# Five warm-up steps of TensorE for eight, and a second level of the 7-for-8 product in the third block

## The chip, the cores and the metric

The kernel runs on one core of a Trainium2 chip, in one launch. A core has a matrix engine (TensorE, "PE" in the profile; its weight loads are listed apart as "PEld"), three engines for elementwise work (VectorE "DVE", ScalarE "ACT", GpSimd "POOL"), an engine that here only issues transfers (SyncE, "SP"), and 16 DMA engines that serve all of them. Each engine takes its own instructions in the order in which the program lists them, and waits on semaphores for the others. The metric is the device time of one execution in microseconds; 2% is the line between "faster", "the same" and "slower".

## The reference, cut to what matters

```python
# attention, for 8 batches x 12 heads, 448 tokens, 64 columns per head, all fp32
q_n, k_n = rmsnorm(q, g_q), rmsnorm(k, g_k)
scores = (1 / sqrt(64)) * q_n @ k_n.T
attn = softmax(scores)                      # along the keys
x = (attn @ v)                              # heads side by side: (8*448, 768)

# bilinear feed-forward, d_model 768, d_ff 1536
a = x @ w_a                                 # (3584, 1536)
b = x @ w_b                                 # (3584, 1536)
out = (a * b) @ w_out                       # (3584, 768)
```

The attention is small beside the three large products. The weights arrive as float64 and are rounded to fp32 on the chip.

## The kernel before: the parts that matter here

A small scheduler in the kernel (`Plan`) records every operation with an estimate of its time and a priority (a lower key goes first), and lays the operations out in one fixed order for each engine before anything runs. A change in the list of operations can thus move others.

The 8 batches are cut into `NB = 4` blocks of two batches (`beta` 0 to 3). For each block `ffn(beta)` makes `h = (x w_a) * (x w_b)` with `quarter_products`, and then `last_product` multiplies `h` by `w_out`. All of them use the 7-for-8 algorithm (Strassen's, in Winograd's form): a product is cut in quarters, and seven products of quarters, with sums before and after, replace eight. The sums are DVE work; the factors on the weights' side are computed once, kept in DRAM (`kept`) and read back by `stream`.

`last_product` takes groups of 128 tokens in pairs: three pairs in an even block, four in an odd one (the tokens left over from both blocks of two make the fourth). For each of the seven factors `f` and each pair, one product of quarters is 6 matmuls of 128x384. In the fourth block, and for five of the seven factors, two pairs are taken together as a group, and a second level of the same algorithm cuts their 12 matmuls into seven products of 3 matmuls of 128x192:

```python
WARM = 8
TWICE = (1, 2, 3, 4, 6)        # factors with a second level
MAKE = 1                       # block in which the second level's weight factors are made
ONCE = NB - 1                  # first block that uses the second level
...
for f in (0, 1, 2, 4, 3, 5, 6):
    stream(beta, 12 + place_of[f], f)
    if beta == MAKE and f in TWICE:
        inner_factors(beta, f)
    if beta >= ONCE and f in TWICE:
        stream_inner(beta, f)
groups = [(0, 1), (2, 3)][:len(pairs) // 2] if beta >= ONCE else []
alone = [t for t in pairs if not any(t in g for g in groups)]

def each(f, a, base, to):
    twice = groups if f in TWICE else []
    for g in twice:
        inner_products(beta, key + place_of[f], f, g, a, base, to, acc, (c_, U_), out_place)
    for t in pairs if not twice else alone:
        product(t, f, a(t), plain(t, base, to))
```

`product` is the plain form, with its result taken by `plain` in one DVE addition (0.56 us each) or a copy on ACT:

```python
for c in ks:                                                 # 6 in all
    nc.tensor.matmul(held["po"][:, 0:HALF], lhsT=a[0]()[:, c], rhs=sts[beta, 12 + place_of[f]][:, c], ...)
```

`inner_products` is the second level (cut to its matmuls and the names of its sums):

```python
factor(0, a10, a11, ALU.add, nx1)                   # four sums of token quarters, on DVE (Si)
factor(1, s(0), a00, ALU.subtract, ...)
factor(2, a00, a10, ALU.subtract, nx)
factor(3, a01, s(1), ALU.subtract, ...)
...
for c in range(MI):                                 # MI = 3, HI = 192; seven such products: a b a d g e g
    nc.tensor.matmul(held[bank], lhsT=x()[:, c], rhs=y(c), ...)
...                                                 # seven to twelve DVE additions behind them (pi, fin, oi)
```

Its weight factors come from `inner_factors` (per `f` eight DVE subtractions into two small buffers, each followed by a store to DRAM) and return by `stream_inner`: four loads per `f`, which take over the attention's buffers and therefore wait until the attention has ended:

```python
tag, bufs = ("ET", 4) if place_of[f] % 2 == 0 else (("v", 2), ("v", 2), ("q", 1), ("k", 1))[n]
...
nc.sync.dma_start(inner[beta, f, n], kept["t"][:, f, n])      # needs "ended": the attention is done
```

A block's `ffn` may be recorded before or after the last attention heads:

```python
if p // (2 * HC) <= ONCE:
    ffn(p // (2 * HC) - 1)
elif p == NC:
    for beta in range(ONCE, NB):
        ffn(beta)
```

At the start, before the first heads have arrived, TensorE runs warm-up steps of four 128x128 matmuls whose results nobody reads:

```python
def warm():
    for x in range(4):
        nc.tensor.matmul(warms[0][:, 0, 0:P], lhsT=ident, rhs=ident, start=True, stop=True)
...
for x in range(WARM):
    op("PE", 0.86, 1e6, warm, ["warm"], ["warm"], mode="full")
```

Of the kernel before, what the change touches and what calls it, by code (L numbers as in the profile page):

```python
# [25 lines left out]
class Plan:  # L26
# [22 lines left out]
    def op(self, engine, us, key, emit, reads=(), writes=(), new=(), mode=None, chain=None, kb=0, lock=False, dmas=1):  # L49
        n, deps, tiles = len(self.ops), set(), set()  # L50
        for t in new:
            self.opener[t] = n
            tiles.add(t)
        for r in reads:
            if r in self.wrote:
                deps.add(self.wrote[r])
            self.read.setdefault(r, []).append(n)
        for w in writes:
            if w in self.wrote:
                deps.add(self.wrote[w])  # L60
            deps.update(self.read.pop(w, ()))
            self.wrote[w] = n
        for x in (*reads, *writes):
            t = x.split("/")[0]
            if t in self.tags:
                deps.add(self.opener[t])
                tiles.add(t)
        deps.discard(n)
        self.ops.append((engine, us, key, emit, deps, mode, chain, kb, tuple(new), tiles, lock, dmas if kb else 0))
        return n  # L70
# [100 lines left out]
def kernel(  # L171
# [112 lines left out]
    NB = B // 2  # L284
# [14 lines left out]
    def fast_body(ld, wk, ps_s, ps_o, ps_mm, dram):  # L299
        plan = Plan()  # L300
        op, tile_of = plan.op, plan.tile
# [3 lines left out]
        HC, NT = HP // 2, S // D  # L305
        NC = B * HC
        STS, XS = 2, 9
        WARM = 8
        TWICE = (1, 2, 3, 4, 6)
        MAKE = 1  # L310
        ONCE = NB - 1
        LOADS = "ACT"
        KEEPS = "ACT"
        APART = 24
# [91 lines left out]
        def stream(beta, n, f=None):  # L406

            st = tile_of(f"st{beta}.{n}", "st", STS)

            def load():  # L410
                t = sts[beta, n] = ld.tile([P, 7, KH * P], FP32, tag="st", name="st", bufs=STS)
                if f is None:
                    nc.sync.dma_start(t.rearrange("p a b -> p (a b)"), kept[n])
                else:
                    nc.sync.dma_start(t[:, 0:MH], kept["o"][:, f])
            reads = [f"kept{n}"] if f is None else [f"kept{len(order) + x}" for x in range(MH)]
            op("SP", 0.5, 6.0 * beta + n / 4, load, reads, [f"{st}/{x}" for x in range(7)] + ["streaming"], new=[st],
               kb=1376 if f is None else 1180)
# [268 lines left out]
        def last_product(beta, h, key):  # L687
# [22 lines left out]
            pairs = range(PAIRS if odd else OWN)  # L710
# [5 lines left out]
            def product(t, f, a, take):  # L716

                po, held = tile_of(f"po{beta}.{t}.{f}", "mm", 2), {}
                for part in range(2):
                    ks = range(part * MH // 2, (part + 1) * MH // 2)  # L720

                    def emit(ks=ks):
                        if ks[0] == 0:
                            held["po"] = ps_mm.tile([P, 512], FP32, tag="mm", name="po")
                        for c in ks:
                            nc.tensor.matmul(held["po"][:, 0:HALF], lhsT=a[0]()[:, c], rhs=sts[beta, 12 + place_of[f]][:, c],  # L726
                                             start=(c == 0), stop=(c == MH - 1))
                    op("PE", len(ks) * HALF / 595, key + place_of[f], emit, a[1] + [f"st{beta}.{12 + place_of[f]}/0"], [po, "ffn"],
                       new=[po] if part == 0 else [], mode="full")
                take(po, lambda: held["po"][:, 0:HALF])  # L730
# [19 lines left out]
            c_, U_ = (lambda t: f"{fin}/c{t}"), (lambda t: f"{fin}/U{t}")  # L750
            for f in (0, 1, 2, 4, 3, 5, 6):
                stream(beta, 12 + place_of[f], f)
                if beta == MAKE and f in TWICE:
                    inner_factors(beta, f)
                if beta >= ONCE and f in TWICE:
                    stream_inner(beta, f)
            groups = [(0, 1), (2, 3)][:len(pairs) // 2] if beta >= ONCE else []
            alone = [t for t in pairs if not any(t in g for g in groups)]

            def each(f, a, base, to):  # L760


                twice = groups if f in TWICE else []
                for g in twice:
                    inner_products(beta, key + place_of[f], f, g, a, base, to, acc, (c_, U_), out_place)
                for t in pairs if not twice else alone:
                    product(t, f, a(t), plain(t, base, to))

            def out_place(t, i):
                return 2 * S * beta + (t + OWN * i) * P if t < OWN else 2 * S * (beta - 1 + i) + 2 * OWN * P  # L770
# [1 line left out]
            def plain(t, base, to):  # L772
                name = lambda y: (c_, U_)[y](t)
                if base is None:
                    return lambda po, ps: op("ACT", 0.5, -1, lambda: nc.scalar.copy(acc(t, to), ps()), [po], [name(to)])
                if not isinstance(to, tuple):
                    return lambda po, ps: op("DVE", 0.6, -1, lambda: nc.vector.tensor_tensor(acc(t, to), acc(t, base), ps(), ALU.add),
                                             [po, name(base)], [name(to)])

                def take(po, ps):  # L780
                    out_(t, *to[:2], base)(po, ps)
                    if len(to) > 2:
                        op("DVE", 0.6, -1, lambda: nc.vector.tensor_tensor(acc(t, to[2]), acc(t, to[2]), ps(), ALU.add),
                           [po], [name(to[2])])
                return take
# [60 lines left out]
        def stream_inner(beta, f):  # L846
            for n in range(4):
                tag, bufs = ("ET", 4) if place_of[f] % 2 == 0 else (("v", 2), ("v", 2), ("q", 1), ("k", 1))[n]
                nm = tile_of(f"ti{beta}.{f}.{n}", tag, bufs)

                def load(n=n, tag=tag, bufs=bufs):
                    shape = {"ET": [P, 2, S], "k": [P, NT, 2, D]}.get(tag, [P, 2, NT * D])
                    t = (wk if tag == "ET" else ld).tile(shape, FP32, tag=tag, name="ti", bufs=bufs)
                    flat = t.rearrange("p a b c -> p (a b c)" if tag == "k" else "p a b -> p (a b)")
                    inner[beta, f, n] = flat[:, 0:MI * HI].rearrange("p (k n) -> p k n", k=MI)
                    nc.sync.dma_start(inner[beta, f, n], kept["t"][:, f, n])
                op("SP", 0.5, 6.0 * beta + (12 + place_of[f]) / 4, load, [f"kt{f}.{n}.0", f"kt{f}.{n}.{MI - 1}", "ended"], [nm], new=[nm], kb=295)
# [247 lines left out]
        def weights(at, after):  # L1105
            for x, n in enumerate(seq):
                if at == GATES[x]:
                    factors(n, x * 0.45 + 1.0, x < 2, [after])
# [5 lines left out]
        for p in range(NC + 1):  # L1114
            if p < NC:
                for nm in "qkv":
                    loads(p, nm)
            if p == 0:
                weights(0, "k0")
                op("SP", 1.0, -1.9, load_gains, [], ["grow"], kb=1, dmas=2)  # L1120
                op("DVE", 0.4, -9, use_gains, [], ["grow"])
                op("DVE", 0.4, 20.0, judge_gains, ["grow"], [])
                spread_gains()
                for x in range(WARM):
                    op("PE", 0.86, 1e6, warm, ["warm"], ["warm"], mode="full")
            if p < NC:
                normalize(p)
                transposes(p)
                scored(p, 0)
                scored(p, 1)  # L1130
            if p > 0:
                if p > WIDE:
                    sums_over_keys(p - 1, None)
                invert(p - 1)
                divide(p - 1)
                if (p - 1) % (2 * HC) == 2 * HC - 2:
                    combine((p - 1) // (2 * HC), 0)
                if p % (2 * HC) == 0:
                    combine(p // (2 * HC) - 1, 1)
                    combine(p // (2 * HC) - 1, 2)  # L1140
# [6 lines that stand above are left out]
            if p < NC:  # L1147
                for j in range(NT):
                    values(p, j)
                    if p < WIDE:  # L1150
                        sums_over_keys(p, j)
                    elif j:
                        add_up(p, j)
                    if j + 2 < NT:
                        scored(p, j + 2)
                put_out(p)
# [130 lines left out]
```

## Time and profile before

The time is 1555.44 us (median of 3 runs, 1555.27 to 1557.61). The profiled execution has a span of 1553.5 us.

| engine | busy us | share of the span | instructions |
|---|---|---|---|
| PE (matmul) | 1515.4 | 98% | 6894 |
| PEld (weight load) | 813.1 | 52% | 6894 |
| DVE | 769.9 | 50% | 1089 |
| ACT | 399.4 | 26% | 647 |
| POOL | 315.0 | 20% | 166 |

| stretch, us | what runs there |
|---|---|
| 0 to 235 | attention of the first block; the weights are loaded, rounded and kept |
| 235 to 394 | the rest of the first block's quarter products |
| 394 to 576 | attention of the second block; the first block's last product |
| 576 to 755 | the second block's quarter products |
| 755 to 962 | attention of the third block; the second block's last product |
| 962 to 1140 | the third block's quarter products |
| 1140 to 1173 | the last heads of the fourth block's attention, with the rest of the quarter products |
| 1173 to 1254 | the third block's last product |
| 1254 to 1443 | the fourth block's quarter products |
| 1443 to 1553 | the fourth block's last product, with the second level |

How to read the lines of a profile: L726 is line 726 of the kernel. An fp32 matmul shows as two records, so "x6" in the trace are three matmuls of the program. The mean duration of one matmul is longer than the distance between two, because they are pipelined: distances are read from the chain of waits, where a row is the start, the length and the number of records. PEclk, in a table of stretches, is the TensorE clock that was granted (1.00 is full). `po` is a plain product of the last product (L726), `pq` a quarter product (L1003), and the seven products of the second level are `a`, `b`, `d`, `g`, `e` (L901). `hraw` and `lraw` hold the weights as loaded, `st` the rounded factors, `ti` the second level's weight factors, `tk` the same while they are made.

### The profile page before, as it was taken

To read this page: it belongs to the slowest core of one execution; us is meant where nothing else is said; L and a number is where in the kernel's file an instruction comes from. 1 tells how busy PE (TensorE), PEld (TensorE's weight loads), DVE (VectorE), ACT (ScalarE), POOL (GpSimd) and SP (SyncE) were. 2 spreads that over 40 slices of the span, in tenths; PEclk is the share of its full clock that TensorE was granted. 3 is DMA by queue.
4 is the path that set the end of the run, shared out by engine and by line. 5 is a ranking of instruction groups with operands and counts; after the bars stand their busy time and mean duration, and the time that the engine had idled before them with its cause. 6 is when DMAs were issued, how large, how long until landed. Compare 5 with 4: busy or idle time off the path is not lost.

```text
span 1553.5 us, 17619 instructions
## 1 busy us (share of the span) xinstructions
PE 1515.4 (98%) x6894; PEld 813.1 (52%) x6894; DVE 769.9 (50%) x1089; ACT 399.4 (26%) x647; POOL 315.0 (20%) x166
## 2 busy tenths in 40 slices
PE   8988999999999999999999999999999999999998
PEld 6654344555444555555444455555545555555796
DVE  4887769888786412222377542222235222222583
ACT  4767662111557200000455400000040000000000
POOL 2426442111255200001244400001110001000000
PEclk9999999999999999999999999999999999999999
DMA  8898445554535551212246445121214432222343
GB/s 236 232 261 244 97 102 182 182 198 153 162 110 122 143 169 71 107 71 95 82 109 164 109 146 174 72 107 71 107 64 149 127 127 90 89 77 95 110 138 110
DMA packets 122528, 204.09 MB, mean 131 GB/s; under 512 B 57157, under 2 KB 105541, under 8 KB 112709
## 3 DMA queue, kind: packets, MB, share of 16 engines
q1 hardware_dynamic: 94372, 149.40, 32.4%
q10 hardware_dynamic: 28064, 53.48, 9.9%
q8 instruction: 56, 0.92, 0.2%
q14 instruction: 36, 0.29, 0.1%
HBM read 160.83 MB, written 41.85 MB: 130 GB/s over the span
## 4 chain that ended last, share of the span: by engine, by line
PE 85%; DMA 4%; DVE 4%; ACT 3%; issue 1%; POOL 1%; SPq 0%; ACTq 0%; DVEq 0%; POOLq 0%
PE pq L1003 49%; PE po L726 18%; PE o L537 6%; PE sc L515 5%; DMA q_sb<-in_q_dram 2%; PE su L573 2%; PE pt L494 2%; ACT ET L521 2%; PE g L901 1%; PE a L901 1%; DVE x L662 1%; PE warm L1094 1%; DMA hraw<-in_moe_w_out_dram 1%; DMA kept_o<-st 1%; PE b L901 1%
## 5 line engine op out<-in xcount | busy, mean ns | idle before, releaser
L1003 PE MATMUL pq<-x,st 128*128 128x448 f32 x2016 | 763.4, 540 | 0.0
L1003 PEld LDWEIGHTS pq<-x,st 128*128 128x128 f32 x2016 | 381.2, 190 | 378.6 <-issue 369.9
L521 ACT ACTIVATE ET<-sc,ms 128x448 f32<-128x448 f32 x336 | 192.8, 636 | 92.9 <-PE sc L515 66.3
L726 PE MATMUL po<-st,hT 128*128 128x384 f32 x624 | 204.8, 487 | 0.0
L537 PE MATMUL o<-ET,v_sb 64*64 64x448 f32 x1344 | 186.3, 551 | 9.2 <-ACT ET L521 8.7
L515 PE MATMUL sc<-qkT 64*64 64x448 f32 x1344 | 177.7, 548 | 17.3 <-ACT ET L521 10.1
L464 POOL TENSOR_TENSOR ms<-ms,expo 128x14 f32<-128x14 f32 x48 | 147.2, 3085 | 205.1 <-DVE ms L462 199.7
L1051 POOL TENSOR_TENSOR hT<-hT,t 128x448 f32<-128x448 f32 x24 | 28.8, 1199 | 746.6 <-DVE t L1049 744.3
L726 PEld LDWEIGHTS po<-st,hT 128*128 128x128 f32 x624 | 117.9, 190 | 84.7 <-issue 3.6
L1025 ACT COPY hT<-pq 128x448 f32<-128x448 f32 x24 | 12.8, 533 | 436.4 <-PE pq L1003 436.4
L515 PEld LDWEIGHTS sc<-qkT 64*64 64x64 f32 x1344 | 59.3, 133 | 93.9 <-issue 34.3
L551 POOL TENSOR_TENSOR sum<-sum,ET 128x896 f32<-128x896 f32 x38 | 81.0, 2131 | 127.5 <-ACT ET L521 76.0
L537 PEld LDWEIGHTS o<-ET,v_sb 64*64 64x64 f32 x1344 | 60.9, 134 | 87.0 <-ACT ET L521 39.5
L726 PE MATMUL po<-st,fin 128*128 128x384 f32 x312 | 105.5, 490 | 0.0
L726 PEld LDWEIGHTS po<-st,fin 128*128 128x128 f32 x312 | 58.3, 190 | 46.6 <-issue 7.8
L551 DVE TENSOR_TENSOR sum<-sum,ET 128x896 f32<-128x896 f32 x57 | 62.4, 1095 | 39.6 <-POOL sum L551 33.9
L746 DVE TENSOR_TENSOR o_sb<-fin,po 128x384 f32<-128x384 f32 x44 | 24.4, 555 | 113.1 <-PE po L726 109.3
L1063 POOL TENSOR_TENSOR hT<-hT,t 128x448 f32<-128x448 f32 x48 | 57.9, 1208 | 51.0 <-DVE t L1060 47.5
L458 DVE TENSOR_REDUCE ms<-sq 128x14 f32<-128x896 f32 x48 | 51.8, 1079 | 24.9 <-ACT sq L456 24.7
L1056 DVE TENSOR_TENSOR hT<-U,pq 128x448 f32<-128x448 f32 x48 | 29.8, 621 | 66.3 <-PE pq L1003 66.3
L1060 DVE TENSOR_TENSOR t<-U,pq 128x448 f32<-128x448 f32 x48 | 29.7, 619 | 61.5 <-PE pq L1003 59.1
L1028 ACT COPY t<-pq 128x448 f32<-128x448 f32 x24 | 12.8, 534 | 176.0 <-PE pq L1003 176.0
(113 smaller groups left out, 1145.2 us busy)
## 6 DMA issues: line engine op xcount, KB each, us to landing
st<-kept SPq DMA_DIRECT2D x36, 1344.0 KB
st<-kept_o SPq DMA_DIRECT2D x28, 1152.0 KB
kept<-st ACTq DMA_DIRECT2D x12, 1344.0 KB
q_sb<-in_q_dram SPq DMA_DIRECT2D x48, 224.0 KB
k_sb<-in_k_dram SPq DMA_DIRECT2D x48, 224.0 KB
v_sb<-in_v_dram SPq DMA_DIRECT2D x48, 224.0 KB
rec<-inv SPq DMA_DIRECT2D x48, 224.0 KB
lraw<-in_moe_w_a_dram ACTq DMA_DIRECT2D x12, 768.0 KB
```

Source lines behind the costliest of these rows:

```text
L458: op("DVE", 1.1, key, lambda: nc.vector.tensor_reduce(rs[p][:, s], xs["sq", nm, p], AX, ALU.add), [sq], [f"{ms}/{nm}"])
L464: lambda: nc.gpsimd.tensor_tensor(msf(), msf(), expo[:, 0:2 * NT * (b - a)], ALU.pow), [], names)
L494: nc.tensor.transpose(t[:, j * P:(j + 1) * P], x[:, j].rearrange("p h d -> p (h d)"), ident)
L515: nc.tensor.matmul(t[low_high[w], e, 0:S], lhsT=qkTs[p][low_high[e], 1, j * P + w * D:j * P + (w + 1) * D], rhs=qkTs[p][low_high[e], 0, w ...
L521: nc.scalar.activation(E[:, e], scs[p, j][:, e, 0:S], AF.Exp, scale=rs[p][:, 1, 2 * j + e:2 * j + e + 1])
L537: nc.tensor.matmul(os_[p][low_high[e], w, 0:S], lhsT=xs["v", p][low_high[w], e, j * D:(j + 1) * D], rhs=ETs[p, j][low_high[w], e], start=( ...
L551: two[e].tensor_tensor(sums[p], sums[p] if j > 1 else ETs[p, 0], ETs[p, j], ALU.add)
L573: nc.tensor.matmul(sus[p][w][low_high[e], :], lhsT=ones[low_high[w], :], rhs=x[low_high[w], e], start=first, stop=last)
L726: nc.tensor.matmul(held["po"][:, 0:HALF], lhsT=a[0]()[:, c], rhs=sts[beta, 12 + place_of[f]][:, c], start=(c == 0), stop=(c == MH - 1))
L901: nc.tensor.matmul(held[bank], lhsT=x()[:, c], rhs=y(c), start=(start and c == 0), stop=(stop and c == MI - 1), skip_group_check=True)
L1003: nc.tensor.matmul(banks[bank][:, 0:S], lhsT=sts[at][:, f, c * P:(c + 1) * P], rhs=quads[x][:, c], start=(start and c == 0), stop=(stop an ...
L1063: lambda i=i, n=n, nm=nm: two[TIMES].tensor_tensor(C(i, n), C(i, n), held[nm], ALU.mult), [t], [hp[i]],
```

## The change

It has three parts. `WARM` goes from 8 to 5, and the scheduler is told that the first three steps take longer (2.5, 1.7 and 1.7 us) than the rest. The second level is also used in the third block (`ONCE = NB - 2`), for all seven factors, for the pairs 0 and 1; pair 2 stays plain. For this the second block makes the weight factors of all seven `f`. And inside `each` the plain product of the pair that stands alone now goes ahead of the group. In the fourth block, the second level stays at the same five factors. The aim of the second part is less matmul work: 21 half-size matmuls in place of 12 for each of the seven factors.

```diff
-        WARM = 8
-        TWICE = (1, 2, 3, 4, 6)
+        WARM = 5
+        TWICE = {NB - 2: (0, 1, 2, 3, 4, 5, 6), NB - 1: (1, 2, 3, 4, 6)}
         MAKE = 1
-        ONCE = NB - 1
+        ONCE = NB - 2
...
                 stream(beta, 12 + place_of[f], f)
-                if beta == MAKE and f in TWICE:
+                if beta == MAKE:
                     inner_factors(beta, f)
-                if beta >= ONCE and f in TWICE:
+                if f in TWICE.get(beta, ()):
                     stream_inner(beta, f)
...
-                twice = groups if f in TWICE else []
+                twice = groups if f in TWICE.get(beta, ()) else []
+                for t in pairs if not twice else alone:
+                    product(t, f, a(t), plain(t, base, to))
                 for g in twice:
                     inner_products(beta, key + place_of[f], f, g, a, base, to, acc, (c_, U_), out_place)
-                for t in pairs if not twice else alone:
-                    product(t, f, a(t), plain(t, base, to))
...
                 for x in range(WARM):
-                    op("PE", 0.86, 1e6, warm, ["warm"], ["warm"], mode="full")
+                    op("PE", (2.5, 1.7, 1.7)[x] if x < 3 else 0.9, 1e6, warm, ["warm"], ["warm"], mode="full")
```

Since `ONCE` also decides when a block's `ffn` is recorded, the third block's `ffn` now stands behind the last head in the list of operations. In the built program TensorE's order is the same up to the third block's attention, but for the start: there 16 warm-up matmuls, then the seven transposes of the first keys, the small gain product, four more warm-up matmuls, and then the transposes of the first queries; before, all 32 warm-up matmuls came first.

## The prediction

> **What bounds the kernel now.** I read the page first: TensorE is busy 98% of the span, and the chain that ended last is 85% TensorE work. So a change counts only if it shortens TensorE's work or closes a gap in it. Then I read the chain in order of time for the two places that the change touches, the third block's last product and the second level in the fourth block.
>
> ```profile
> 1172.76 81.27 PE po L726 x252
> 1254.03 189.42 PE pq L1003 x504
> 1443.45 15.48 PE po L726 x48
> 1458.93 0.97 PE a L901 x6
> ...
> 1464.78 1.18 PE g L901 x6
> 1465.97 0.97 PE a L901 x6
> ```
>
> The first row is the whole stage that gets the second level: 81.27 us for 7 factors x 3 pairs, 3.87 us per plain product and pair, without a gap. The third gives the same price (15.48 / 4 = 3.87). The last three bound one group of the second level that nothing disturbs: from 1458.93 to 1465.97 are 7.04 us for what costs 2 x 3.87 = 7.74 us in the plain form.
>
> For the start I read the timeline of the first 30 us and stretches of 2 us:
>
> ```profile
> 10.42 1.13 DVE L468 TENSOR_TENSOR qn<-q_sb,ms 128x896 f32<-128x896 f32 x1
> 11.47 0.93 PE L494 MATMUL pt<-ident,k_sb 128*128 128x128 f32 x7
> 12.75 0.39 ACTq L379 DMA_DIRECT2D hraw<-in_moe_w_out_dram  x1
> 14.81 1.74 PE L515 MATMUL sc<-qkT 64*64 64x448 f32 x16 [1.19 <-ACT qkT L501]
> 23.41 1.58 ACT L271 ACTIVATE st<-hraw 128x1536 f32<-128x1536 f32 x1 [5.28 <-DMA hraw<-in_moe_w_out_dram]
> 26.41 2.29 PE L537 MATMUL o<-ET,v_sb 64*64 64x448 f32 x8 [4.54 <-ACT ET L521]
> ```
>
> ```profile
> 10.00:12.00 2.00, 2.00 (x20) 2.00 (x19) 1.42 (x3) 0.00 (x0) 1.99 (x2) 1.00 0.28 64
> 12.00:14.00 2.00, 1.62 (x13) 1.20 (x11) 0.00 (x0) 1.22 (x3) 0.98 (x1) 1.00 0.45 125
> ...
> 22.00:24.00 2.00, 0.00 (x0) 0.00 (x0) 0.00 (x0) 0.59 (x1) 0.00 (x0) 1.00 0.92 307
> 24.00:26.00 2.00, 0.00 (x0) 0.00 (x0) 0.96 (x1) 2.00 (x3) 0.00 (x0) 0.61 1.04 403
> 26.00:28.00 2.00, 1.59 (x9) 1.06 (x13) 1.95 (x2) 1.93 (x4) 0.00 (x0) 0.50 1.10 332
> ```
>
> (Columns of the stretches: PE, PEld, DVE, ACT, POOL busy, granted clock, DMA share, GB/s.) The eight warm-up steps run from 1.37 to 11.63 and the key transposes stand behind them. ACT's gain copy and the first weight load on ACT's queue wait in turn for TensorE, so the DMA engines are nearly idle from 10 to 14 us. The load lands late, ACT blocks on it for 5.28 us, TensorE has nothing for 4.54 us, and at about 24.5 us its clock falls to half until about 31.
>
> **What the Trainium skill says.** "TensorE: Matmul & The Clock Gate", section "Back-to-back issue gap", gives N/2.4 + 2.5 ns between matmuls when warm, and "FP8 and Floating Point Precision", section "TensorE Precision Notes", gives four passes for true fp32. My estimate from the two is 4 x 82.5 = 330 ns for 192 columns and 4 x 162.5 = 650 ns for 384. The trace has 0.97 / 3 = 323 and 15.48 / 24 = 645 ns: it agrees, and half-size matmuls are not dearer per column. "What's actually happening" in the first page says that the clock is halved after about 3.4 us of idleness; here it fell during a gap of 4.5 us, while gaps of 1.2 us left it alone. "VectorE: DVE Perf Modes", section on the TRN2 errata, gives (N+151)/0.96 ns for an fp32 tensor_tensor: 557 ns for 384 elements, 357 for 192; the rows of the second level's sums have 554 and 352 to 358.
>
> **The change part by part.**
>
> *Second level in the third block.* Per factor, the group costs 7.04 for 7.74 us: 0.70 us less. Times seven: 4.9 us, all on TensorE and so on the path, if nothing stalls. The stage becomes 7 x (3.87 + 7.04) = 76.4 us.
>
> *What this adds to DVE there.* Counted from the new order between the first token sum and the end of the stage: 28 token sums x 0.555 = 15.5; the additions behind the groups 20.7 (1.75 for f=0, 3.0 for each of five, 3.95 for f=5); nine sums between factors x 0.95 = 8.6; seven plain takes 3.9; the attention's last divisions and combinations, and the last sums of `h`, about 8. Together 57 of 76 us, 74%. Before, it was
>
> ```profile
> 1172.60:1254.00 81.40, 81.40 (x254) 48.01 (x253) 31.25 (x47) 1.62 (x4) 1.13 (x1) 1.00 0.42 137
> 1473.00:1503.50 30.50, 28.50 (x170) 27.16 (x169) 26.38 (x57) 1.28 (x4) 0.00 (x0) 1.00 0.48 158
> ```
>
> The second row is the fourth block's worst stretch, two groups for f=2 and f=4: DVE 26.38 of 30.5 us. Undisturbed it should take 4 x 7.04 = 28.15 us, so about 2.4 us are lost there. The third block has half as much second-level work and a plain product of 3.87 us ahead of each group for DVE to get its sums done, so I expect no such hole.
>
> *What it adds to the DMAs.* 28 more loads of 288 KB, 8.3 MB, on 137 GB/s x 81.4 us = 11.2 MB: about 19.4 MB in 76.4 us, 254 GB/s. Scaled from a share of 0.42 that is near 0.78. The st load of a factor must land within one factor, 10.9 us, and the traffic of a factor with stores (2.36 MB and 0.6 MB) needs about 9 us at the 325 GB/s which share and rate imply. Tight, not over. For holes of both kinds I put +0.7 us.
>
> *More weight factors.* Sixteen more DVE subtractions, 8 x 0.55 + 8 x 0.35 = 7.2 us, with 16 stores. They are made in the second block's last product and, for f=0, inside the third block's attention, where TensorE waits for others now and then (idle 0.6 of the 57 us to 811, 2.6 of the next 71). They have priority over the attention's sums and share two small buffers with the quarter products. With the reshuffle of the attention's order around them I put +1.0 us, give or take two.
>
> *Warm-up.* A step is 8 records; at 11 per 2 us at first and 20 at the end, the first four steps end near 7 us. The keys land near 8.0 (ACT starts on them at 8.04), so their transposes run at 8.0 in place of 11.47. The weight load is issued near 9.2 in place of 12.75: 3.5 us earlier, into the empty stretch. The queries are ready at 11.55, so the first scores start near 13.55 in place of 14.81: 1.25 us. How much survives until 235 us depends on who leads there. If it is the attention chain, 1.25; if the DMAs (share 0.8 to 1.1 over most of the first 150 us), 3.5; if the earlier landing also spares the idle 4.5 us and the 4 to 5 us at half clock, up to 6. I take 3.0.
>
> Sum: -4.9 - 3.0 + 0.7 + 1.0 = -6.2 us, 1549.2 us.
>
> **The rivals.**
>
> *A: the second level is paid back in the third block.* DVE sums or `ti` loads end last, as they did in the fourth block. For it: 2.4 us were lost there, and DMA demand nearly doubles. Against it: 74% DVE, plain products in between, and the first eight `ti` loads were issued between 1156 and 1167 us even before, some 10 us ahead of need. It would make the stage 79 to 82 us and the kernel 1552 to 1555.
>
> *B: the start doesn't carry.* The weights' chain (DVE 88% busy from 25 to 125 us) absorbs what the first 25 us gain, or the thinner warm-up leaves TensorE at half clock for the first heads. Against the latter: after step four it still transposes, and idles under 2 us at a time. It would leave 1551 to 1553.
>
> *C: the new order hurts the attention of the third block.* DVE is in order; a `tk` subtraction that waits for its buffer's store holds up the sums that attention needs. Before, such waits came to 5.7 us in five cases. It would add 2 to 5 us: 1551 to 1554.
>
> *D: the start gives everything* and removes the half-clock stretch: 1545 to 1546.
>
> **Range and chances.** A to D move it by 3 to 5 us each, independently. I take 1543.5 to 1554.5 as the range. 2% would be 31 us, six times what any part can give, and no added work comes near it in the other direction: chances 0.01 faster, 0.98 the same, 0.01 slower.
>
> **What would show it.** In the profile after: the stage of the third block's last product between the quarter products takes 76 to 78 us, with groups of 7.0 us; the first weight load is issued before 10 us; no half clock, or a shorter one, near 25 us; the transition from the first attention to the unbroken run of quarter products (235.6 us before) comes about 3 us earlier; the stretch from there to the start of the third block's last product is as long as before, within 2 us. It is wrong if groups in the third block show waits on `ti` or `Si`, if the 235 us mark hasn't moved, or if the third block's attention has grown by over 3 us.

## The result, and the profile after

The kernel after takes 1548.32 us (median of 4 runs, 1543.98 to 1550.43), the kernel before beside it 1556.11 us (4 runs, 1555.27 to 1557.61). The ratio is 0.9945, 95% interval [0.9919, 0.9972]: 7.8 us less, within 2%. A second measurement of the same kernel (7 runs) gave 1550.27 us and a ratio of 0.9964 [0.9951, 0.9977]. The profiled execution took 1550.43 us with a span of 1548.6, the longest of the four, so the two profiles differ by 4.9 us and not by 7.8.

The start comes first. These are rows of the timeline of the kernel after (start, length, engine and line; in brackets the idle time before and what ended it), and then its stretches of 2 us (columns as before: PE, PEld, DVE, ACT, POOL busy, granted clock, DMA share, GB/s):

```profile
9.23 0.39 ACTq L379 DMA_DIRECT2D hraw<-in_moe_w_out_dram  x1
13.65 1.73 PE L515 MATMUL sc<-qkT 64*64 64x448 f32 x16 [1.16 <-ACT qkT L501]
16.84 1.67 ACT L271 ACTIVATE st<-hraw 128x1536 f32<-128x1536 f32 x1
```

```profile
10.00:12.00 2.00, 0.77 (x7) 0.57 (x6) 1.27 (x2) 0.19 (x1) 2.00 (x2) 1.00 1.01 258
12.00:14.00 2.00, 0.84 (x9) 0.46 (x11) 0.00 (x0) 1.01 (x1) 0.88 (x1) 1.00 1.02 418
...
24.00:26.00 2.00, 2.00 (x25) 1.46 (x21) 1.97 (x2) 0.64 (x3) 1.81 (x1) 1.00 1.02 418
```

The load goes out at 9.23 in place of 12.75, and the DMA engines are full from 10 us on, where they had shares of 0.28 and 0.45. ACT's first conversion of weights (`st<-hraw`) starts at 16.84 in place of 23.41 and carries no bracket: the data are there when its turn comes. So the chain ACT blocked, TensorE idle for 4.54 us, clock halved is gone whole; PEclk is 1.00 in every stretch shown. Scores begin only 1.16 us earlier than before.

The second level in the third block's last product, in the chain of waits of the kernel after (start, length, what), and the stage as one stretch:

```profile
1185.68 0.97 PE a L901 x6
...
1191.53 1.19 PE g L901 x6
1192.72 3.87 PE po L726 x12
...
1237.92 7.74 DMA out_dram<-oi
...
1247.88 1.24 PE g L901 x6
```

```profile
1170.60:1249.10 78.50, 76.56 (x380) 63.56 (x379) 52.93 (x109) 4.62 (x11) 1.38 (x2) 1.00 0.75 243
```

A group takes 1192.72 - 1185.68 = 7.04 us, as in the fourth block. But the stage took 78.6 us and not 76.4. A 7.74 us row of DMA stands in the chain near its end: stores of results hold up the last group. The timeline shows the hole, with SyncE's issues ahead of it (SPq):

```profile
1235.72 0.32 SPq L413 DMA_DIRECT2D st<-kept  x1
1237.40 3.32 SPq L1076 DMA_DIRECT2D out_dram<-oi  x4
1245.78 0.35 DVE L942 TENSOR_TENSOR oi<-fin,a 128x192 f32<-128x192 f32 x1 [2.83 <-DMA out_dram<-oi]
1247.88 1.24 PE L901 MATMUL g<-ti,hT 128*128 128x192 f32 x6 [1.50 <-DVE oi L957]
```

The sums of f=6 need the output buffers (`oi`) that f=5's group has filled and that are still being stored. DVE waits 2.83 us for them, its sums come late, and the last `g` waits 1.50 us for one of them. Ahead of the four stores, SyncE has issued the load of a whole factor of the quarter products that follow (`st<-kept`, 1344 KB).

For the whole program I cut each profile at the same marks of TensorE's work: the start of the unbroken run of quarter products, the second block's quarter products, the third block's, and the start and end of the third block's last product. All times in us; "third attention" is the sum of the stretches before and after the third block's quarter products.

| kernel | start mark | third attention | last product, third block |
|---|---|---|---|
| before | 235.6 | 239.9 | 81.4 |
| after (two profiles) | 230.8, 229.8 | 243.4, 243.2 | 78.6, 78.7 |

The rest differs by about 1 us: from the start mark to the second block's quarter products 340.8 and 339.9, the second and the third block's quarter products 178.1 each in both, and after the last product 299.5 each.

### The profile page after: what moved, and what is told of

It is laid out like the page before. It is cut to its first block, busy times and chain, and to the rows that moved or that the text cites. A ratio compares the mean times of both kernels' runs of the same rounds, so it can differ in the third digit from the quotient of the medians.

```text
span 1548.6 us, 18051 instructions
## 1 busy us (share of the span) xinstructions
PE 1506.9 (97%) x6996; PEld 822.6 (53%) x6996; DVE 813.7 (53%) x1179; ACT 400.7 (26%) x654; POOL 314.1 (20%) x166
## 4 chain that ended last, share of the span: by engine, by line
PE 82%; DMA 7%; DVE 5%; ACT 3%; issue 1%; POOL 1%; SPq 1%; ACTq 0%; DVEq 0%; POOLq 0%
PE pq L1003 48%; PE po L726 16%; PE sc L515 5%; PE o L537 4%; DMA q_sb<-in_q_dram 2%; PE g L901 2%; PE a L901 2%; ACT ET L521 2%; PE pt L494 2%; DMA rec<-inv 1%; PE b L901 1%; PE su L573 1%; PE e L901 1%; PE d L901 1%; DMA lraw<-in_moe_w_b_dram 1%
## 5 line engine op out<-in xcount | busy, mean ns | idle before, releaser
L726 PE MATMUL po<-st,hT 128*128 128x384 f32 x504 | 166.4, 487 | 0.0
L726 PEld LDWEIGHTS po<-st,hT 128*128 128x128 f32 x504 | 95.0, 190 | 67.9 <-issue 3.9
L551 POOL TENSOR_TENSOR sum<-sum,ET 128x896 f32<-128x896 f32 x38 | 81.4, 2141 | 139.1 <-ACT ET L521 97.0
L726 PE MATMUL po<-st,fin 128*128 128x384 f32 x264 | 89.9, 490 | 0.0
L726 PEld LDWEIGHTS po<-st,fin 128*128 128x128 f32 x264 | 49.1, 190 | 39.0 <-issue 7.0
L746 DVE TENSOR_TENSOR o_sb<-fin,po 128x384 f32<-128x384 f32 x36 | 20.0, 554 | 80.2 <-PE po L726 72.4
```

The costliest lines, as they stand in the source:

```text
L551: two[e].tensor_tensor(sums[p], sums[p] if j > 1 else ETs[p, 0], ETs[p, j], ALU.add)
```

## The experiments

Each run has its own interval against the kernel before, measured beside it.

**1 and 2: the two halves of the change.** The warm-up alone is the kernel before with

```diff
-        WARM = 8
+        WARM = 5
-                    op("PE", 0.86, 1e6, warm, ...)
+                    op("PE", (2.5, 1.7, 1.7)[x] if x < 3 else 0.9, 1e6, warm, ...)
```

> The kernel before with only the warm-up changed (5 steps, with the scheduler's new estimates for the first three). Theory 1 (the start gives what the profile after shows): the unbroken run of quarter products begins near 231 us in place of 235.6, and all later stages keep their lengths, so the kernel takes 1550 to 1551.5 us, ratio 0.9965 to 0.9975. Rival (the start doesn't carry to the end, it is absorbed in a later attention stretch): 1554 to 1556 us.

and the second level alone is the kernel after with the reverse of this edit.

> The changed kernel with the old warm-up of 8 steps. Theory 1 (the parts add): the quarter products begin near 235.6 us, the stretch from the third block's attention to its last product is 3 to 5 us longer than before, the last product with the second level is 2.8 us shorter, and the last heads of the fourth block's attention 1.9 us shorter: 1555 to 1556 us, no gain. Rival (the second level gives its 4.9 us): 1551 us.

Measured: warm-up alone 1549.31 us (4 runs), ratio 0.9955 [0.9938, 0.9971]; second level alone 1556.96 us (12 runs), ratio 1.0006 [0.9994, 1.0017]. In the profiles the start mark is at 227.4 and 237.1, the last product at 81.4 and 78.6. So nearly the whole gain is the warm-up's: 0.0045 x 1555.87 = 7.0 us (4.5 to 9.6 by the interval), more than the 0.9965 to 0.9975 expected. The second level shortens its stage by 2.8 us and yet gains nothing: the third attention takes most of it back (241.8 us for 239.9).

**3: without f=0.** The third block's second level for six factors, and the weight factors of f=0 not made:

```diff
-        TWICE = {NB - 2: (0, 1, 2, 3, 4, 5, 6), ...
+        TWICE = {NB - 2: (1, 2, 3, 4, 5, 6), ...
-                if beta == MAKE:
+                if beta == MAKE and f in TWICE[NB - 2]:
```

> The changed kernel without the second level for f=0 in the third block, so that its weight factors aren't made either. Theory (making f=0's factors inside the third block's attention costs about 3.3 us there, as the DVE waits for the two small buffers): the stretch from the end of the second block's quarter products to the start of the third's shrinks from 212 to 208 or 209 us, the last product grows by 0.3 to 0.7 us, the kernel takes 1.5 to 3.5 us less than the changed one. Rival (the stretch is longer because the order of the attention moved, whatever the factors do): it stays at 211 to 213 us and the kernel is no faster.

Measured: 1548.3 us, 0.9951 [0.9935, 0.9968]; third attention 240.06 us. In time that can't be told from the kernel after, but the stretch is back at its old length.

**4: the same work, at a lower priority.** The subtractions that make the weight factors go behind the attention's sums:

```diff
-    op("DVE", 0.16 + size / 980, -0.5, emit, [st] + ...
+    op("DVE", 0.16 + size / 980, 40.0, emit, [st] + ...
```

> The changed kernel with the weight factors' subtractions at a low priority (behind the attention's DVE work) in place of a high one; the same work. Theory (the factors hold up the attention because they go first): the stretch shrinks to 208 to 210 us and the kernel gains 1.5 to 3.5 us on the changed one. Rival (it is the amount of DVE work and stores, not its place): no change, 211 to 213 us.

Measured: 1549.75 us, 0.9963 [0.9948, 0.9977]; third attention 243.59. The priority is not the lever; the order changes, the stretch stays as long.

**5: the kernel after once more,** in more rounds, beside the next three.

> The changed kernel once more, for a narrower interval and a second profile. Theory (the warm-up carries nearly all, the second level's gain in its stage is lost again to the third block's attention): the ratio is that of the warm-up alone, 0.9945 to 0.9960; the last product of the third block again takes 78.5 to 79 us with one hole of about 1.5 us before its last product, the stretch of the third block's attention 210 to 213 us. Rival (the second level is worth 3 us or more on top): ratio below 0.9940.

Measured: the 1550.27 us named above, ratio 0.9964, just over the range for the warm-up alone.

**6: the first weight load early, by its priority.** The kernel before, with the load's key so low that the scheduler takes it first:

```diff
-                op(LOADS, 0.45, key - 0.75, load, after, [f"{row}/{part}"], kb=768)
+                op(LOADS, 0.45, key - 0.75 if n != 15 else -20.0, load, after, [f"{row}/{part}"], kb=768)
```

> The kernel before with all eight warm-up steps, but with the first two weight loads put ahead of the gain copy and the second key's squares on ACT's queue, so that they are issued near 8 us, when the first keys have landed, in place of 12.75; TensorE's first scores stay at 14.8. Theory (the earlier weight load is what the shorter warm-up gave): ACT no longer blocks for 5 us, TensorE's clock stays full, the unbroken run of quarter products begins at 228 to 230 us, the ratio is 0.995 to 0.997. Rival (the 1.2 us of the attention chain and the warm-up matmuls themselves are what counts): it begins at 234 to 236 us, the ratio is 0.999 to 1.001.

Measured: 1570.01 us, 1.0096 [1.0079, 1.0112]: within 2%, but some 14 us longer, against both expectations. Two rows of its timeline and a stretch of 25 us:

```profile
5.36 0.90 ACTq L379 DMA_DIRECT2D hraw<-in_moe_w_out_dram  x2
19.07 0.95 ACT L456 ACTIVATE sq<-q_sb 128x896 f32<-128x896 f32 x1 [2.04 <-DMA q_sb<-in_q_dram]
```

```profile
100.00:125.00 25.00, 14.72 (x123) 8.09 (x122) 22.51 (x27) 13.32 (x18) 8.19 (x3) 0.84 1.02 309
```

The load went out at 5.36, not near 8, while the first heads were still on their way, and the second head's queries then kept ACT waiting. And the scheduler, given another key, laid out the whole first attention anew: TensorE is busy 14.72 of the 25 us from 100 on, where it was busy 22.65 before, and the start mark is at 249.9. The run changes too much at once and decides nothing about the load. Experiments 9 and 10 mend it.

**7: the group ahead of the plain product again,** within each factor; all else as after.

```diff
                 twice = groups if f in TWICE.get(beta, ()) else []
-                for t in pairs if not twice else alone:
-                    product(t, f, a(t), plain(t, base, to))
                 for g in twice:
                     inner_products(...)
+                for t in pairs if not twice else alone:
+                    product(t, f, a(t), plain(t, base, to))
```

> The changed kernel with the old order in each factor: the group of the second level first, then the plain product of the pair that stands alone. Theory (the plain product of 3.87 us covers the DVE's sums for the group behind it): the last product of the third block grows from 78.6 to 82 to 86 us, with waits of b on Si at f=0 and at f=4, the kernel is 3 to 7 us slower than the changed one. Rival (DVE has enough slack at 74% either way): 78 to 80 us.

Measured: 1544.3 us (4 runs), 0.9927 [0.991, 0.9945], where I had expected it slower. The end of its stage in the chain of waits:

```profile
1236.34 0.97 PE e L901 x6
1237.32 1.17 PE g L901 x6
1238.48 3.87 PE po L726 x12
```

The last `g` follows the `e` at once (1236.34 + 0.97 = 1237.31); the hole is gone. The timeline of SyncE shows what has changed ahead of it:

```profile
1227.93 2.52 SPq L1076 DMA_DIRECT2D out_dram<-oi  x4
1231.09 0.33 SPq L413 DMA_DIRECT2D st<-kept  x1
```

The stores now go out ahead of the factor's load; in after it was the other way round. A factor's buffer is free for the next load when its last reader has run. With the group last that is the group's own `e`, before its sums are done and stored (in after the load's issue is released by `e`); with the plain product last it is the plain product, 4.8 us after the group's `e`. From the end of the third block's quarter products to the start of the fourth's this order takes 108.25 us, after's 109.73: 1.48 us less, the hole of 1.50.

**8: without f=5.** The other way to keep that hole from opening: f=5, whose sums are the longest and whose stores hold the buffers, stays plain.

```diff
-        TWICE = {NB - 2: (0, 1, 2, 3, 4, 5, 6), ...
+        TWICE = {NB - 2: (0, 1, 2, 3, 4, 6), ...
-                if beta == MAKE:
+                if beta == MAKE and f in TWICE[NB - 2]:
```

> The changed kernel without the second level for f=5 in the third block. Theory (the hole before the last product is f=6 waiting for the two output buffers that f=5's stores still hold): the hole of 1.5 us goes, f=5 costs 0.7 us more, the last product takes 77.5 to 78 us. Rival (the hole is the DMA engines' load of 0.75 and comes wherever the stores are): it stays near f=6 and the stage takes 79 to 79.5 us.

Measured: 1547.36 us, 0.9943 [0.9924, 0.9962]. The stage takes 77.59 us with one group less, where after takes 78.64; no DMA row is left in the stage's chain. With one group less TensorE has 0.70 us more to do, and the stage is 1.05 us shorter.

**9 and 10: the load moved, and nothing else.** Experiment 6 had moved everything. Here the finished order of all engines is kept, and only the two issues of the first weight load are given out at another place in it. In 9, the kernel before with eight steps, they stand ahead of ACT's gain copy:

```diff
+            def take():
+                for start in first:          # the first weight load's two issues
+                    start()
+                nc.scalar.copy(gain, held["pg"][:, 0:1])
-            op("ACT", 0.2, -9, lambda: nc.scalar.copy(gain, held["pg"][:, 0:1]), [pg], ["gain"])
+            op("ACT", 0.2, -9, take, [pg], ["gain"])
```

> The kernel before with its eight warm-up steps; only the first weight load's two issues stand ahead of the gain copy on ACT's queue instead of behind the copy of the transposed keys, so that they should go out near 8 us in place of 12.75. The order of everything else on every engine is that of before. Theory L (the warm-up's gain comes from the earlier weight load): the half-clock stretch near 25 us is gone, the unbroken run of quarter products begins at 227 to 231 us, the time is near 1549 to 1551 and the ratio 0.9955 to 0.997. Theory S (it comes from TensorE's earlier transposes and scores): start at 234 to 238, half clock still there, ratio 0.999 to 1.001.

In 10, the kernel of the warm-up alone with five steps, they stand behind the copy of the transposed queries:

```diff
                        nc.scalar.activation(qkTs[p][:, 0]..., AF.Copy, scale=gain[:, 0:1])
+                        if p == 0:
+                            for start in first:
+                                start()
```

> The kernel of the warm-up alone (five steps, new estimates); only the first weight load's two issues stand behind the scaled copy of the transposed queries, so that they should go out near 12.6 us in place of 9.2, as late as in the kernel before. Key transposes near 8 us and first scores near 13.65 stay. The order of everything else stays. Theory L: start at 234 to 238 with the half-clock stretch back, ratio 0.999 to 1.001. Theory S: start at 227 to 231, ratio 0.995 to 0.997.

Rows of the timeline of 9, with one of its stretches:

```profile
7.97 0.92 ACTq L379 DMA_DIRECT2D hraw<-in_moe_w_out_dram  x2
13.78 1.73 PE L517 MATMUL sc<-qkT 64*64 64x448 f32 x16 [1.16 <-ACT qkT L503]
16.97 1.64 ACT L271 ACTIVATE st<-hraw 128x1536 f32<-128x1536 f32 x1
```

```profile
24.00:26.00 2.00, 2.00 (x28) 1.50 (x24) 1.97 (x2) 0.38 (x1) 1.91 (x1) 1.00 0.99 409
```

and of 10:

```profile
12.69 0.93 ACTq L379 DMA_DIRECT2D hraw<-in_moe_w_out_dram  x2
13.73 1.73 PE L520 MATMUL sc<-qkT 64*64 64x448 f32 x16 [1.16 <-ACT qkT L503]
21.72 1.58 ACT L271 ACTIVATE st<-hraw 128x1536 f32<-128x1536 f32 x1 [4.67 <-DMA hraw<-in_moe_w_out_dram]
24.72 1.13 PE L542 MATMUL o<-ET,v_sb 64*64 64x448 f32 x5 [3.93 <-ACT ET L526]
```

```profile
26.00:28.00 2.00, 2.00 (x16) 1.35 (x12) 1.97 (x3) 0.24 (x1) 1.43 (x1) 0.50 1.00 227
```

The scores begin at 13.78 and 13.73, alike. What differs is the load, at 7.97 and 12.69, and with it all the rest: in 9 no wait at `st<-hraw` and full clock, in 10 a wait of 4.67 us, TensorE idle for 3.93 and half clock. The times follow the load, not the number of steps: eight steps with the load ahead 1548.93 us (8 runs), 0.9972 [0.9961, 0.9983], a gain of 4.4 us, the ratio just short of the range expected; five steps with the load late 1553.45 us (14 runs), 0.9995 [0.9984, 1.0006], no gain at all. Start marks: 228.6, as expected, and 232.2, 1.8 short of the range. The profile of 10 has a span of 1549.9 us and so shows one of its fastest executions (1549.7 to 1559.29), which may be why. In 9 the 64 records of warm-up took 9.27 us, in the profile before 10.27, so that 9 had early scores as well; it is 10, with scores as early and the load late, that tells the two apart. Whether the earlier transposes add a little (0.9955 for five steps with the early load against 0.9972 here) the intervals, which overlap, leave open.

**11 and 12: what could beat both.** In 11 the edits of 3 and 7 together; 12 is the kernel of 7 once more.

> The kernel after, with the group ahead of the plain product within a factor again, and without the second level for f=0 in the third block (and without its factors): six of seven factors. If both gains are real and add: third block's attention near 207 plus the group-first stage at 107 to 109.5, and about 1541 to 1544 us, ratio 0.991 to 0.993. If the gain of the group-first order was scatter beyond its 1.5 us in the stage: 1546 to 1548, ratio 0.994 to 0.995. If leaving out f=0 gives nothing in time, as in the run that left it out alone (1548.3): the same as the group-first order alone, 1544.3.

> The kernel after with the group ahead of the plain product within a factor, once more and in more rounds: its order differs from after's in the third block's last product alone, where the profiles show 1.5 us less. If that is all it gains: 1546.5 to 1548.5 us, ratio 0.995 to 0.9965. If the 4 to 6 us by which it beat after in its first measurement are real: 1543.5 to 1545.5, ratio 0.992 to 0.994.

Measured: 1545.76 us (6 runs), 0.9947 [0.9935, 0.9959], and 1545.27 us (6 runs), 0.9945 [0.9931, 0.9959]. The ratio of 11 lies in the second of the ranges expected, its time just below it: leaving f=0 out shortens the third attention (241.12 us) and costs one group's gain, and added nothing to 7 that could be measured. The time of 12 lies in the range for a gain beyond the hole, its ratio between the two. The group-first order was thus measured at 0.9927 and 0.9945, the change at 0.9945 and 0.9964: it is ahead of it by about 0.2% or 3 us, of which the profiles explain 1.5. The rest is not settled; the two pairs of intervals would allow for the 1.5 alone.

## Why the prediction was right, point by point

The total was foreseen as -6.2 us and came out at -7.8, and at -5.6 in the second measurement (0.0036 x 1556.23): both within the range. Its terms were off by more than the total, in both directions: +2.6 us for the two costs and -4.0 for the warm-up. That they largely cancel is luck.

| term of the sum | predicted | measured | from |
|---|---|---|---|
| second level, TensorE's work | -4.9 | -4.9 | groups of 7.04 us for 7.74 |
| holes in its stage | +0.7 | +2.1 | 81.4 to 78.6 us is -2.8; -2.8 + 4.9 |
| weight factors, third attention | +1.0 | +2.2 | means of profiles, below |
| warm-up | -3.0 | -7.0 | warm-up alone, 0.9955 |
| sum | -6.2 | -7.6 | before to after: -7.8 and -5.6 |

*Second level, the price of a group: right.* 7.04 us to the hundredth, in the group shown. DVE is busy 52.93 of 78.50 us, 67% for 74% estimated, and the DMA share is 0.75 for 0.78: neither is the bound, as argued against rival A.

*Holes: under-sized.* The step that failed is "so I expect no such hole". It weighed DVE's load, the `ti` loads and the st load, and TensorE waited for none of the loads; but it never asked when the output buffers of one group come free for the next. The swap within `each` was given credit ("a plain product of 3.87 us ahead of each group for DVE to get its sums done"), and it is this swap that puts a 1344 KB load ahead of the stores and opens the 1.50 us hole. With the group first, the hole is gone (experiment 7), and without f=5, too (8); that it is the load ahead of the stores, and not another part of the order, is read from the rows and was not tried alone. The remaining 0.6 us are small waits at f=0, f=2 and f=5.

*Weight factors: under-sized, in the direction of rival C.* The third attention takes 239.9, 242.7, 240.7, 239.9 and 240.8 us in the five profiles without the third block's second level (before, 1, 6, 9, 10), a mean of 240.8. With f=0's factors made it takes 243.4, 243.2, 241.8, 243.6 and 243.0 (after twice, 2, 4, 8), a mean of 243.0. Without them it takes 240.1 and 241.1 (3, 11), as if there were no second level at all. So about 2.2 us, and they come with f=0, the one factor whose making is added while attention runs; f=5's factors, the other ones added, are made after the attention (from 885 us on) and cost nothing that can be seen. The 242.7 of experiment 1 holds a stretch at half clock that the other four lack:

```profile
832.40:835.80 3.40, 3.40 (x24) 1.07 (x16) 2.71 (x5) 1.30 (x3) 2.78 (x2) 0.50 0.32 116
```

Without that profile the mean is 240.3, and the cost 2.7 us. Where it arises, the chain of waits of the kernel after and three rows of its timeline suggest, at the beginning of this attention:

```profile
757.34 3.55 DMA kept_t<-tk
760.92 2.09 DVE tk L840 x2
763.00 2.44 DMA kept_t<-tk
...
767.43 0.38 SPq L842
...
768.48 3.87 DMA rec<-inv
```

```profile
760.92 2.33 DVE L840 TENSOR_TENSOR tk<-st 128x192 f32<-128x192 f32 x2 [0.40 <-DMA kept_t<-tk]
765.53 1.84 DVE L840 TENSOR_TENSOR tk<-st,tk 128x192 f32<-128x192 f32 x2 [1.01 <-DMA kept_t<-tk]
773.35 0.98 PE L515 MATMUL sc<-qkT 64*64 64x448 f32 x8 [0.53 <-ACT ET L521]
```

Two subtractions need the stores of 3.55 and 2.44 us that empty their two buffers. DVE does attention's sums meanwhile, so that it idles only 0.40 and 1.01 us for them. The next stores' issue (L842) then stands on SyncE's queue ahead of the transfer `rec<-inv` (224 KB) that the next division needs. This is rival C's mechanism, but TensorE loses only 0.53 us here. In the whole stretch ahead of the third block's quarter products it idles 4.8 us, for 3.2 before and 3.1 in experiment 3; 1.05 us of that stand 100 to 110 us into the stretch, where no factor is made and the kernel before shows no idle time. So the cost of f=0 is shown by leaving it out (3); by which path it comes, the waits or the order, is not. Putting the subtractions later (4) didn't help. By the criterion of the prediction ("grown by over 3 us") the pair before and after, 239.9 to 243.4, counts against it. The stretch ahead of the quarter products alone grew from 207.0 to 212.3, but the transposes of a head have moved into it (42 records for 35), and the stretch behind them shrank from 32.9 to 31.1.

*Warm-up: under-sized by more than half.* Three options were set out, 1.25, 3.5 and "up to 6", and "I take 3.0" is the step that failed. The last was the case, rival D: the start gives everything (its 1545 to 1546 us for the whole failed on the two costs). The clue stood in the profile of before, in the rows quoted there: 4.54 us idle, and behind them 4.9 us of work at half clock (26.41 to 31.29), cost more than the 3.5 us by which the load is late. The start mark is at 235.6 and 237.1 with eight steps and a late load, and at 226.1 to 232.3 in nine profiles with five steps and an early one, a mean of 228.7. Rival B's first half, that DVE's 88% would absorb it, falls.

"TensorE: Matmul & The Clock Gate", section "What's actually happening", in the Trainium skill has the clock go to half after an idle window of about 3.4 us, windows that run on by themselves: the gaps of 4.54 us (before) and 3.93 us (10) had it follow, the gaps of 0.38 and 0.73 us that are left near 28 us in after and in 9 didn't. So the late load costs twice, and a load that is early enough saves both. But no single long gap is needed, as two stretches of experiment 8 show:

```profile
11.00:14.40 3.40, 1.54 (x15) 1.08 (x19) 0.65 (x1) 1.01 (x1) 2.07 (x1) 1.00 0.95 370
14.40:17.80 3.40, 3.40 (x24) 1.20 (x20) 0.00 (x0) 2.29 (x5) 0.00 (x0) 0.50 1.10 248
```

There TensorE's gaps were 1.24 and 1.16 us, it was busy 1.54 of the 3.40 us, and the clock went to half for the first scores; in 11 the same came at 13.1 us. The kernel after has the same gaps and kept its clock. So rival B's other half, the thinner warm-up leaving TensorE at half clock for the first heads, came true in two of the nine profiles, and the start mark of 8 is the latest of the nine, 232.3.

*The mechanism of the warm-up: right, but named by its lesser half.* It is not the three steps that cost time. They matter because ACT's gain copy waits for a product behind them, and the load is issued behind that copy. Experiment 9 takes 4.4 of the 7.0 us with all eight steps in place, and experiment 10 loses it all with five.

*The five marks set out:* load before 10 us (9.23), no half clock, and the start mark earlier (4.8 us in after's profile, for 3) came true. The groups of 7.0 us came true too, but the stage took 78.6 us, just over the 76 to 78 given. From the start mark to the third block's last product it is 937.2 us before and 1170.64 - 230.8 = 939.8 after: 2.6, just over the 2 allowed. The last two are the two under-sized costs.

## What to carry to other kernels

When a transfer is issued on a compute engine's queue, look for what the instructions ahead of it wait for: here two issues went out at 12.75 us behind one blocked copy and at 7.97 ahead of it, and by experiments 9 and 10 that is worth about 4 to 6 us, as much as the arithmetic saved in a whole stage (4.9). When an algorithm saves TensorE work, price not only its sums and its loads but ask of each group when the output buffers of the one before come free, and what is issued ahead of their stores. To test the place of one instruction, move that one in the finished order; a changed priority lets a scheduler move hundreds.

## What the runs showed that was not expected

Skipping the second level for one factor made its stage faster (77.59 us for 78.64): the stores of the longest group were what the next one had waited for.

Programs with the same order in the third attention take 239.9 to 240.8 us for it, and 242.7 where 3.4 us at half clock fell into it; the time of one kernel differs by 9 us and more from run to run (1549.7 to 1559.29 for experiment 10). A second measurement of the same kernel moved its ratio from 0.9945 to 0.9964 and, in the group-first order, from 0.9927 to 0.9945; at half a per cent, one measurement of four runs ranks nothing.
